# Grouped-query attention: K of a head pair loaded with 8 KB rows, the score matmuls on four tiles, P written with a step of 2

## The chip, the core and the metric

The kernel runs on one core of a Trainium2 chip. The core has five engines that each work through their own list of instructions: PE (TensorE, matmuls and transposes into PSUM), DVE (VectorE), ACT (ScalarE), POOL (GpSimd) and SP (SyncE, which here only issues transfers). They meet at semaphores. Sixteen DMA engines move data between the memory outside (HBM) and the 128 partitions of the on-chip memory (SBUF). The metric is the device time of one execution in microseconds (us). Before the change it is 353.08 us, the median of three runs (351.69 to 353.13).

## The reference: what is computed

```
B, Hq, Hkv, Sq, Sk, D = 16, 32, 8, 16, 2048, 128        # q, k, v in bf16
k = jnp.repeat(k, 4, axis=1); v = jnp.repeat(v, 4, axis=1)
scores = jnp.einsum("bhqd,bhkd->bhqk", q, k) * D ** -0.5
p = softmax(scores, axis=-1)
out = jnp.einsum("bhqk,bhkd->bhqd", p, v)
```

There are 16 x 8 = 128 KV heads. Four query heads of 16 rows share each, so a KV head has a block of 64 query rows against 2048 keys of 128 numbers. K and V of one KV head are 512 KB each; all of K and V is 134 MB, and q and the output are 2 MB each.

## The kernel before

Two KV heads make a *pair*: 64 + 64 query rows fill 128 partitions, and there are `NP` = 64 pairs. All loops run over pairs p.

**Loads (SP, L158 to L206).** For each step t, SP issues K of pair t (`load_k`, L160), every eighth step a block of Q, V of pair t-4 (`load_v`, L170), and the store of the result of pair t-12 (`store`, L190). K has `NK` = 6 buffers `Kn`, V has 8. K of pair p waits until the transposes of pair p-6 are done (L163), V of pair p until PV of pair p-8 is done (L173). The view `kf` (L87) puts head g, partition a at 2048 consecutive numbers, that is 4 KB: partition a of `Kn` holds keys 16a to 16a+15 of the first head and then the same of the second. A transfer of 1 MB thus consists of 256 pieces of 4 KB. K of pair 0 comes as two transfers of 512 KB with a semaphore each (L164 to L166). V has the same layout (L88); V of the last pair comes in two halves of 2 KB rows (L178). The store of a pair writes 128 rows of 256 B.

**Transposes of K (DVE, `kt`, L286).** Scores need K with the 128 numbers of a key along the partitions. DVE transposes 32x32 blocks of 4-byte words (two bf16 at a time), one instruction of 1024 words per partition for each head, from `Kn` to `KT` (two buffers). After it, the partitions 32r to 32r+31 hold the keys that lay in those partitions of `Kn`: block r of 32 partitions has 512 keys of head 0 and 512 of head 1.

**Scores (PE, op "S", L229 to L250).** The query block comes transposed in `QT`, in four slices (`acc`) of 32 numbers each, repeated in every 32-partition block. For each `acc`, 8 matmuls of 32 rows x 64 columns x 512 keys go to 8 different tiles of the PE array: row block r (4 of them) times column half g (head g, 2 of them). Output: bank r of `S_ps`, partition half g. The four `acc` add up in PSUM. S of pair p waits for both transposes of pair p and, since there is only one `S_ps`, for DVE to have read the scores of pair p-1 (`sem_max`).

**Softmax.** DVE copies `S_ps` to `Sneg` (L307), scaled by -scale and with the row minimum into `nbias`. ACT (L336) takes exp of `Sneg` plus bias, sums the rows and writes P in bf16, two neighbours to each 4-byte word. PE transposes P in 4-byte words (op "PT", L259, two halves), ACT copies the result to `PT` (L346). PE multiplies `PT` by V (op "PV", L275, 32 matmuls, three pairs behind), and ACT scales by the reciprocal of the row sum (L356).

**Order.** PE's and ACT's lists are written out by the loop at L115 to L136: PE does S(p+1), PV(p-3), PT(p), and in four of each eight steps a part of the next Q block (QT, L227). DVE's list (L300 to L315) is, for each p: Sneg(p), the reciprocal of p-1 (L298), the two transposes of pair p+2.

Of the kernel before, what the change touches and what calls it, by code (L numbers as in the profile page):

```python
# [5 lines left out]
ACT = mybir.ActivationFunctionType  # L6
ALU = mybir.AluOpType
BF16 = mybir.dt.bfloat16
# [16 lines left out]
def bass_standalone__gqa_softmax__sampling_kernel(  # L25
# [21 lines left out]
    iota_t = sb("iota_t", [128, 128], I32)  # L47
    ident = sb("ident", [128, 128], BF16)
    ident4 = sb("ident4", [128, 128], F32)
    Kn = [sb(f"Kn{i}", [128, 2, J * 128], BF16) for i in range(NK)]  # L50
    Vb = [sb(f"Vb{i}", [128, 2, J, 128], BF16) for i in range(NV)]
    KT = [sb(f"KT{i}", [128, 2, J * 64], F32) for i in range(NKT)]
    Qn = [sb(f"Qn{i}", [128, 8, 128], BF16) for i in range(NQ)]

    QT = [sb(f"QT{i}", [128, 4, 1024], BF16) for i in range(2)]
# [10 lines left out]
    O_ps = ctx.enter_context(nc.psum_tensor("O_ps", [128, 512], F32))  # L66

    sem_id = sem("sem_id")
    sem_k0 = [sem(f"sem_k0{g}") for g in range(2)]
    sem_k = [sem(f"sem_k{i}") for i in range(NK)]  # L70
    sem_v = [sem(f"sem_v{i}") for i in range(NV)]
    sem_vl = [sem(f"sem_vl{i}") for i in range(2)]
# [11 lines left out]

    qf = q.rearrange("b h s d -> (b h s) d")
    of = out.rearrange("b h s d -> (b h s) d")
    kf = k.rearrange("b h s d -> (b h) (s d)").rearrange("g (a x) -> a g x", a=128)  # L87
    vf = v.rearrange("b h s d -> (b h) (s d)").rearrange("g (a x) -> a g x", a=128)  # L88


# [58 lines left out]
    with nc.Block() as block:  # L149
# [8 lines left out]
        @block.sync  # L158
        def _(sp):
            def load_k(p):  # L160
                s = p % NK
                if p >= NK:
                    sp.wait_ge(sem_kt, 2 * (p - NK) + 2)  # L163
                if p == 0:  # L164
                    for g in range(2):
                        sp.dma_start(Kn[s][:, g, :], kf[:, g, :]).then_inc(sem_k0[g], 16)  # L166
                else:
                    sp.dma_start(Kn[s][:, :, :], kf[:, 2 * p:2 * p + 2, :]).then_inc(sem_k[s], 16)  # L168

            def load_v(p):  # L170
                s = p % NV
                if p >= NV:
                    sp.wait_ge(sem_pv, p - NV + 1)  # L173
                if p < NP - 1:
                    dst = Vb[s][:, :, :, :].rearrange("a g j d -> a g (j d)")
                    sp.dma_start(dst, vf[:, 2 * p:2 * p + 2, :]).then_inc(sem_v[s], 16)  # L176
                    return
                for x in range(2):  # L178
                    dst = Vb[s][:, :, 8 * x:8 * (x + 1), :].rearrange("a g j d -> a g (j d)")
                    src = vf[:, 2 * p:2 * p + 2, 1024 * x:1024 * (x + 1)]  # L180
                    sp.dma_start(dst, src).then_inc(sem_vl[x], 16)  # L181

            def load_q(c):
                s = c % NQ
                if c >= NQ:
                    sp.wait_ge(sem_st, last_q[c - NQ, 3] + 1)
                src = qf[1024 * c:1024 * (c + 1), :].rearrange("(a j) d -> a j d", j=8)
                sp.dma_start(Qn[s][:, :, :], src).then_inc(sem_q[s], 16)

            def store(p):  # L190
                s = p % NO
                sp.wait_ge(sem_nm, p + 1)
                sp.dma_start(of[128 * p:128 * (p + 1), :], Osb[s][:, :]).then_inc(sem_o[s], 16)  # L193

            for t in range(NP + SLAG + 1):
                if t < NP:
                    load_k(t)
                for c in range(NQC):
                    if t == max(0, 8 * c - QLEAD):
                        load_q(c)  # L200
                if 0 <= t - VLAG < NP:
                    load_v(t - VLAG)
                if 0 <= t - SLAG < NP:
                    store(t - SLAG)
            for s in range(NO):
                sp.wait_ge(sem_o[s], 16 * (NP // NO))  # L206

        @block.tensor
        def _(pe):
# [6 lines left out]
            for op in pe_prog:  # L216
                if op[0] == "QT":
                    _, c, i, u = op
                    if i == 0:
                        pe.wait_ge(sem_q[c % NQ], 16 * (c // NQ + 1))  # L220
                    free(u)
                    dst = stage_ap(u).bitcast(BF16)
                    src = Qn[c % NQ][:, :, :].rearrange("p j (b c e) -> p j b e c", b=2, e=2)
                    b, e = divmod(i, 2)
                    for j in range(8):
                        for r in range(4):
                            ins = pe.transpose(dst[32 * r:32 * (r + 1), 128 * j:128 * (j + 1)], src[:, j, b, e, :], ident[:, :])  # L227
                    ins.then_inc(sem_st, 1)
                elif op[0] == "S":  # L229
                    _, p = op  # L230
                    pe.wait_ge(sem_kt, 2 * p + 2)
                    if p >= 1:
                        pe.wait_ge(sem_max, p)
                    c, i = divmod(p, 8)
                    if i == 0:
                        pe.wait_ge(sem_ev, last_q[c, 3] + 1)
                    kt = KT[p % NKT][:, :, :].bitcast(BF16).rearrange("p g (t b x e) -> p g b e t x", t=J // 2, b=2, e=2)
                    qt = QT[c % 2]
                    for acc in range(4):
                        b, e = divmod(acc, 2)  # L240
                        for r in range(4):
                            rows = slice(32 * r, 32 * (r + 1))
                            for g in range(2):
                                ins = pe.matmul(  # L244
                                    S_ps[64 * g:64 * (g + 1), 512 * r:512 * (r + 1)],
                                    qt[rows, acc, 128 * i + 64 * g:128 * i + 64 * (g + 1)],
                                    kt[rows, g, b, e, :, :],
                                    start=(acc == 0), stop=(acc == 3),
                                )
                    ins.then_inc(sem_s, 1)  # L250
                elif op[0] == "PT":
                    _, p, h, u = op
                    if h == 0:
                        pe.wait_ge(sem_exp, p + 1)
                    free(u)
                    dst = stage_ap(u)
                    for t in range(4):
                        x = 4 * h + t
                        ins = pe.transpose(dst[:, 128 * t:128 * (t + 1)], P[p % 2][:, 128 * x:128 * (x + 1)], ident4[:, :])  # L259
                    ins.then_inc(sem_st, 1)  # L260
                elif op[0] == "PV":
                    _, p = op
                    pe.wait_ge(sem_ev, last_p[p, 1] + 1)
                    if p < NP - 1:
                        pe.wait_ge(sem_v[p % NV], 16 * (p // NV + 1))
                    if p >= NP - 3:
                        pe.wait_ge(sem_max, NP)
                    elif p >= 1:
                        pe.wait_ge(sem_nm, p)
                    pt = PT[p % NPT][:, :, :].bitcast(BF16).rearrange("p t (q e) -> p t e q", e=2)  # L270
                    for j in range(J):
                        if p == NP - 1 and j % 8 == 0:
                            pe.wait_ge(sem_vl[j // 8], 16)
                        for g in range(2):
                            ins = pe.matmul(  # L275
                                o_ap(p)[64 * g:64 * (g + 1), :],
                                pt[:, j // 2, j % 2, 64 * g:64 * (g + 1)],
                                Vb[p % NV][:, g, j, :],
                                start=(j == 0), stop=(j == J - 1),
                                skip_group_check=True,  # L280
                            )
                    ins.then_inc(sem_pv, 1)

        @block.vector
        def _(dve):
            def kt(p, g):  # L286
                if p == 0:
                    dve.wait_ge(sem_k0[g], 16)
                else:
                    dve.wait_ge(sem_k[p % NK], 16 * (p // NK + (1 if p % NK else 0)))  # L290
                dve.transpose(  # L291
                    KT[p % NKT][:, g, :].rearrange("p (t b a e) -> p t e b a", t=J // 2, b=2, e=2),
                    Kn[p % NK][:, g, :].bitcast(F32).rearrange("p (t e b c) -> p t e b c", e=2, b=2, c=32),
                ).then_inc(sem_kt, 1)

            def recip(p):
# [22 lines left out]
        def _(act):  # L319
            for op in act_prog:  # L320
# [9 lines left out]
                elif op[0] == "exp":  # L330
                    _, p = op
                    act.wait_ge(sem_max, p + 1)
                    if p >= 2:
                        act.wait_ge(sem_st, last_p[p - 2, 1] + 1)

                    act.activation(  # L336
                        P[p % 2][:, :].bitcast(BF16).rearrange("p (t r x) -> p t r x", t=8, r=4),
                        Sneg[p % 2][:, :].rearrange("p (r t x) -> p t r x", t=8, r=4), ACT.Exp,
                        bias=nbias[:, p:p + 1], scale=-1.0, accum_out=rowsum[:, p:p + 1],
                    ).then_inc(sem_exp, 1)  # L340
                elif op[0] == "pe":
# [44 lines left out]
```

## Time and profile before

| | us |
|---|---|
| median of three runs | 353.08 |
| the profiled execution: its time | 352.63 |
| its span, first to last instruction | 350.4 |
| PE busy | 243.3 |
| DVE busy | 296.3 |
| ACT busy | 255.6 |

The mean granted clock of PE is 0.937 of full. 139.22 MB are moved in 45525 packets. The page of the profile has the busy time of each engine, the span in 40 slices (digits are tenths), the DMA queues, the chain of work that ended last, and the groups of instructions with their number, busy time, mean duration in ns, and the idle time before them with what ended it. Other views are the list of waits, the timeline, and a table of stretches of time with the busy time of each engine, the share of DMA time and the rate.

### The profile page before, as it was taken

The page shows a single profiled execution, that of the slowest core. Times are in us where ns is not written, and L with a number is a line of the kernel's source. Part 1 is how long each engine was busy: PE and PEld are TensorE (multiplying, and loading weights), DVE is VectorE, ACT ScalarE, POOL GpSimd, SP SyncE. Part 2 cuts the span into 40 slices and gives each one's busy share as a digit, 9 for nine tenths or more (in the row PEclk, how much of TensorE's full clock was granted, in tenths as well). Part 3 has the DMA queues.
Part 4 walks back from the last instruction along what each step waited for, and adds up shares of the span by engine and source line. Part 5 has one row for each costly group of instructions (what it writes and reads, how often), then busy time and mean ns, then how long its engine had stood idle before and what let it go on. Part 6 is the DMA issues. An engine that isn't in the chain of part 4 may idle for free.

```text
span 350.4 us, 12631 instructions
## 1 busy us (share of the span) xinstructions
PE 243.3 (69%) x5632; PEld 173.5 (50%) x5632; DVE 296.3 (85%) x320; ACT 255.6 (73%) x353; POOL 1.4 (0%) x7
## 2 busy tenths in 40 slices
PE   2578876778667775687649666676775776697675
PEld 2246544546445543365436544454563554465454
DVE  2899999978789887889888897898888888988980
ACT  2578887877758785678757976578957689676575
POOL 1000000000000000000000000000000000000000
PEclk9769999998989999899998999899988999988899
DMA  7999999999999999999999999999999999999983
GB/s 280 416 408 409 406 408 405 412 411 408 414 410 410 412 409 411 410 413 408 408 412 411 409 412 408 410 415 406 411 412 410 410 389 410 412 411 411 409 342 117
DMA packets 45525, 139.22 MB, mean 397 GB/s; under 512 B 11424, under 2 KB 11424, under 8 KB 45472
## 3 DMA queue, kind: packets, MB, share of 16 engines
q1 hardware_dynamic: 45472, 138.42, 99.5%
q8 instruction: 44, 0.72, 0.8%
q14 instruction: 9, 0.07, 0.1%
HBM read 136.31 MB, written 2.10 MB: 395 GB/s over the span
## 4 chain that ended last, share of the span: by engine, by line
DMA 75%; DVE 10%; SPq 6%; issue 5%; PE 2%; ACT 1%
DMA Kn<-in_k_dram 70%; DVE KT L291 8%; DMA Vb<-in_v_dram 4%; SPq L176 3%; DVE Sneg L307 2%; SPq L193 2%; DMA Qn<-in_q_dram 1%; ACT QT L326 1%; SPq L168 1%; PE S_ps L244 1%; PE O_ps L275 0%; PE ST_ps L227 0%; SPq L181 0%; SPq L166 0%; ACT O L356 0%
## 5 line engine op out<-in xcount | busy, mean ns | idle before, releaser
L291 DVE STREAM_TRANSPOSE KT<-Kn 128x1024 f32<-128x1024 f32 x128 | 151.8, 1225 | 43.6 <-DMA Kn<-in_k_dram 43.5
L336 ACT ACTIVATE P<-Sneg,nbias 128x2048 bf16<-128x2048 f32 x64 | 128.1, 2001 | 37.4 <-DVE Sneg L307 37.0
L307 DVE TENSOR_SCALAR_CACHE_REDUCE Sneg<-S_ps 128x2048 f32<-128x2048 f32 x64 | 144.2, 2253 | 1.8 <-PE S_ps L244 1.8
L244 PE MATMUL S_ps<-KT,QT 32*64 32x512 bf16 x2048 | 81.3, 425 | 87.5 <-DVE Sneg L307 75.2
L244 PEld LDWEIGHTS S_ps<-KT,QT 32*64 32x64 bf16 x2048 | 33.7, 109 | 113.5 <-issue 102.7
L346 ACT ACTIVATE PT<-ST_ps 128x512 f32<-128x512 f32 x128 | 69.9, 596 | 21.4 <-PE ST_ps L259 21.4
L259 PE MATMUL ST_ps<-ident,P 128*128 128x128 f32 x512 | 73.1, 288 | 8.9 <-ACT P L336 8.6
L275 PEld LDWEIGHTS O_ps<-Vb,PT 128*64 128x64 bf16 x1952 | 63.1, 119 | 30.3 <-issue 28.8
L275 PE MATMUL O_ps<-Vb,PT 128*64 128x128 bf16 x1952 | 73.7, 233 | 1.2 <-issue 1.0
L259 PEld LDWEIGHTS ST_ps<-ident,P 128*128 128x128 f32 x512 | 57.5, 145 | 18.1 <-ACT P L336 13.6
L356 ACT ACTIVATE O<-O_ps,rrec 128x128 bf16<-128x128 f32 x61 | 22.3, 366 | 25.7 <-PE O_ps L275 25.0
L326 ACT ACTIVATE QT<-ST_ps 128x1024 bf16<-128x1024 bf16 x32 | 32.4, 1024 | 5.6 <-PE ST_ps L227 5.5
L227 PE MATMUL ST_ps<-ident,Qn 128*32 128x128 bf16 x1024 | 21.4, 233 | 6.4 <-DMA Qn<-in_q_dram 6.4
L227 PEld LDWEIGHTS ST_ps<-ident,Qn 128*32 128x32 bf16 x1024 | 16.3, 103 | 11.3 <-issue 10.9
L298 DVE RECIPROCAL rrec<-rowsum 128x1 f32<-128x1 f32 x64 | 10.1, 158 | 2.3 <-ACT P L336 2.3
L336 ACT ACTIVATION_READ_ACCUMULATOR P<-Sneg,nbias 128x1 f32 x64 | 12.1, 188 | 0.0
L307 DVE DVE_READ_ACCUMULATOR Sneg<-S_ps 128x1 f32 x64 | 5.3, 83 | 0.0
L275 PE MATMUL S_ps<-Vb,PT 128*64 128x128 bf16 x96 | 3.4, 220 | 0.7 <-DMA Vb<-in_v_dram 0.6
L275 PEld LDWEIGHTS S_ps<-Vb,PT 128*64 128x64 bf16 x96 | 2.9, 110 | 1.2 <-DMA Vb<-in_v_dram 0.7
L356 ACT ACTIVATE O<-S_ps,rrec 128x128 bf16<-128x128 f32 x3 | 1.1, 369 | 2.0 <-PE S_ps L275 2.0
L326 ACT ACT_TABLE_LOAD x1 | 1.3, 1283 | 0.7 <-PEq L371 0.7
L155 POOL TENSOR_SCALAR ident<-iota_t 128x128 bf16<-128x128 int32 x1 | 0.5, 534 | 0.1
(6 smaller groups left out, 1.2 us busy)
## 6 DMA issues: line engine op xcount, KB each, us to landing
Kn<-in_k_dram SPq DMA_DIRECT2D x63, 1024.0 KB, 15.0
Vb<-in_v_dram SPq DMA_DIRECT2D x63, 1024.0 KB, 16.3
Qn<-in_q_dram SPq DMA_DIRECT2D x8, 256.0 KB, 14.6
out_dram<-O SPq DMA_DIRECT2D x64, 32.0 KB, 13.9
Kn<-in_k_dram SPq DMA_DIRECT2D x2, 512.0 KB, 4.1
Vb<-in_v_dram SPq DMA_DIRECT2D x2, 512.0 KB, 13.4
```

The source lines that it names most:

```text
L176: sp.dma_start(dst, vf[:, 2 * p:2 * p + 2, :]).then_inc(sem_v[s], 16)
L227: ins = pe.transpose(dst[32 * r:32 * (r + 1), 128 * j:128 * (j + 1)], src[:, j, b, e, :], ident[:, :])
L244: ins = pe.matmul(S_ps[64 * g:64 * (g + 1), 512 * r:512 * (r + 1)], qt[rows, acc, 128 * i + 64 * g:128 * i + 64 * (g + 1)], kt[rows, g, b, ...
L259: ins = pe.transpose(dst[:, 128 * t:128 * (t + 1)], P[p % 2][:, 128 * x:128 * (x + 1)], ident4[:, :])
L275: ins = pe.matmul(o_ap(p)[64 * g:64 * (g + 1), :], pt[:, j // 2, j % 2, 64 * g:64 * (g + 1)], Vb[p % NV][:, g, j, :], start=(j == 0), stop ...
L291: dve.transpose(KT[p % NKT][:, g, :].rearrange("p (t b a e) -> p t e b a", t=J // 2, b=2, e=2), Kn[p % NK][:, g, :].bitcast(F32).rearrange ...
L298: dve.reciprocal(rrec[:, p:p + 1], rowsum[:, p:p + 1]).then_inc(sem_rec, 1)
L307: dve.tensor_scalar(Sneg[p % 2][:, :], S_ps[:, :], -scale, None, op0=ALU.mult, op1=ALU.min, accum_out=nbias[:, p:p + 1],).then_inc(sem_max, 1)
L326: act.activation(QT[c % 2][:, i, :].rearrange("p (a j) -> p a j", j=8), stage_ap(u).bitcast(BF16).rearrange("p (j a) -> p a j", j=8), ACT. ...
L336: act.activation(P[p % 2][:, :].bitcast(BF16).rearrange("p (t r x) -> p t r x", t=8, r=4), Sneg[p % 2][:, :].rearrange("p (r t x) -> p t r ...
L346: act.activation(PT[p % NPT][:, 4 * h:4 * (h + 1), :].rearrange("p t q -> p (t q)"), stage_ap(u), ACT.Copy,).then_inc(sem_ev, 1)
L356: act.activation(Osb[p % NO][:, :], o_ap(p), ACT.Copy, scale=rrec[:, p:p + 1]).then_inc(sem_nm, 1)
```

## The change

K of a pair is read as one megabyte that is cut into 128 equal rows: partition a gets 8 KB, that is 32 consecutive keys. The first head fills the partitions 0 to 63, the second 64 to 127. Pair 0 is no longer loaded in two halves, and its two semaphores go. The two transposes of a pair now take the first and the second half of every row (16 of the 32 keys) of both heads, and write every second 4-byte word of `KT`. Row blocks 0 and 1 of `KT` hold only keys of head 0, row blocks 2 and 3 only keys of head 1. So a row block meets only one column half: for each `acc` there are two groups (`u`) of four matmuls of the same size as before, and in a group the row blocks r and r+2 write the same bank of `S_ps`, on different partition halves. Number and sizes of the matmuls stay. The keys lie in another order along `Sneg`; so that P keeps the pairs of neighbours that V's layout asks for, exp writes its bf16 numbers with a step of 2.

```diff
-    Kn = [sb(f"Kn{i}", [128, 2, J * 128], BF16) for i in range(NK)]
+    Kn = [sb(f"Kn{i}", [128, 2 * J * 128], BF16) for i in range(NK)]
-    KT = [sb(f"KT{i}", [128, 2, J * 64], F32) for i in range(NKT)]
+    KT = [sb(f"KT{i}", [128, 2 * J * 64], F32) for i in range(NKT)]
-    kf = k.rearrange("b h s d -> (b h) (s d)").rearrange("g (a x) -> a g x", a=128)
+    kf = k.rearrange("b h s d -> (b h s d)").rearrange("(n a x) -> n a x", n=NP, a=128)
...
-                if p == 0:
-                    for g in range(2):
-                        sp.dma_start(Kn[s][:, g, :], kf[:, g, :]).then_inc(sem_k0[g], 16)
-                else:
-                    sp.dma_start(Kn[s][:, :, :], kf[:, 2 * p:2 * p + 2, :]).then_inc(sem_k[s], 16)
+                sp.dma_start(Kn[s][:, :], kf[p]).then_inc(sem_k[s], 16)
...
-                    kt = KT[p % NKT][:, :, :].bitcast(BF16).rearrange("p g (t b x e) -> p g b e t x", t=J // 2, b=2, e=2)
+                    kt = KT[p % NKT][:, :].bitcast(BF16).rearrange("p (t b y e) -> p b e t y", t=J // 2, b=2, e=2)
...
-                        for r in range(4):
-                            rows = slice(32 * r, 32 * (r + 1))
-                            for g in range(2):
+                        for u in range(2):
+                            for r in range(4):
+                                rows = slice(32 * r, 32 * (r + 1))
+                                g, h = divmod(r, 2)
                                 ins = pe.matmul(
-                                    S_ps[64 * g:64 * (g + 1), 512 * r:512 * (r + 1)],
+                                    S_ps[64 * g:64 * (g + 1), 512 * (2 * h + u):512 * (2 * h + u + 1)],
                                     qt[rows, acc, 128 * i + 64 * g:128 * i + 64 * (g + 1)],
-                                    kt[rows, g, b, e, :, :],
+                                    kt[rows, b, e, 4 * u:4 * (u + 1), :],
                                     start=(acc == 0), stop=(acc == 3),
                                 )
...
-            def kt(p, g):
-                if p == 0:
-                    dve.wait_ge(sem_k0[g], 16)
-                else:
-                    dve.wait_ge(sem_k[p % NK], 16 * (p // NK + (1 if p % NK else 0)))
+            def kt(p, x):
+                dve.wait_ge(sem_k[p % NK], 16 * (p // NK + 1))
                 dve.transpose(
-                    KT[p % NKT][:, g, :].rearrange("p (t b a e) -> p t e b a", t=J // 2, b=2, e=2),
-                    Kn[p % NK][:, g, :].bitcast(F32).rearrange("p (t e b c) -> p t e b c", e=2, b=2, c=32),
+                    KT[p % NKT][:, :].rearrange("p (t b e a x) -> p x e t b a", t=J // 2, b=2, e=2, x=2)[:, x, :, :, :, :],
+                    Kn[p % NK][:, :].bitcast(F32).rearrange("p (x t e b c) -> p x e t b c", x=2, e=2, b=2, c=32)[:, x, :, :, :, :],
                 ).then_inc(sem_kt, 1)
...
-                        P[p % 2][:, :].bitcast(BF16).rearrange("p (t r x) -> p t r x", t=8, r=4),
-                        Sneg[p % 2][:, :].rearrange("p (r t x) -> p t r x", t=8, r=4), ACT.Exp,
+                        P[p % 2][:, :].bitcast(BF16).rearrange("p (t h y e) -> p t h e y", t=8, h=2, e=2),
+                        Sneg[p % 2][:, :].rearrange("p (h t e y) -> p t h e y", t=8, h=2, e=2), ACT.Exp,
```

More of the change, by code (lines that the diff above doesn't have):

```diff
@@ L68, in bass_standalone__gqa_softmax__sampling_kernel @@
     sem_id = sem("sem_id")
-    sem_k0 = [sem(f"sem_k0{g}") for g in range(2)]
     sem_k = [sem(f"sem_k{i}") for i in range(NK)]
```

## The prediction

> **What bounds the kernel now.** I read the page's first three parts, then the chain that ended last, the groups and the waits, and last two tables: the timeline of single pairs and the rates of stretches of time. The page (busy time, slices, queue, chain):
>
> ```profile
> PE 243.3 (69%) x5632; PEld 173.5 (50%) x5632; DVE 296.3 (85%) x320; ACT 255.6 (73%) x353; POOL 1.4 (0%) x7
> ...
> DMA  7999999999999999999999999999999999999983
> ...
> DMA packets 45525, 139.22 MB, mean 397 GB/s; under 512 B 11424, under 2 KB 11424, under 8 KB 45472
> ...
> q1 hardware_dynamic: 45472, 138.42, 99.5%
> ...
> DMA 75%; DVE 10%; SPq 6%; issue 5%; PE 2%; ACT 1%
> ```
>
> The DMA engines are full from the second slice to the 38th, and 75% of the chain is loads. No compute engine is full; DVE is nearest. All 45472 packets are under 8 KB: by pieces, 16384 for K, 16384 + 256 for V, 1024 for Q, 8192 of 256 B for the stores, and 16 small ones for each of the 202 transfers make exactly that number. The waits confirm the chain:
>
> ```profile
> DVE KT L291 <- DMA Kn<-in_k_dram: 43.5, 54, 4.4
> ```
>
> DVE, the busiest engine, idles 43.5 us in total for K to land. The groups that the change touches:
>
> ```profile
> L291 DVE STREAM_TRANSPOSE KT<-Kn 128x1024 f32<-128x1024 f32 x128 | 151.8, 1225 | 43.6 <-DMA Kn<-in_k_dram 43.5
> L336 ACT ACTIVATE P<-Sneg,nbias 128x2048 bf16<-128x2048 f32 x64 | 128.1, 2001 | 37.4 <-DVE Sneg L307 37.0
> L307 DVE TENSOR_SCALAR_CACHE_REDUCE Sneg<-S_ps 128x2048 f32<-128x2048 f32 x64 | 144.2, 2253 | 1.8 <-PE S_ps L244 1.8
> L244 PE MATMUL S_ps<-KT,QT 32*64 32x512 bf16 x2048 | 81.3, 425 | 87.5 <-DVE Sneg L307 75.2
> ```
>
> And the table of stretches (length, busy time of PE, PEld, DVE, ACT, POOL, then PE's clock, DMA share, GB/s). Up to 48 us no store runs yet; from 60 to 280 us everything runs; after 334 us K has all landed and only V and stores are left, and near 338 us V comes in its 2 KB rows:
>
> ```profile
> 18.00:48.00 30.00, 23.57 (x543) 15.83 (x544) 30.00 (x35) 25.36 (x35) 0.00 (x0) 0.91 1.03 408
> 60.00:280.00 220.00, 153.94 (x3624) 110.08 (x3624) 189.71 (x206) 164.23 (x226) 0.00 (x0) 0.95 1.03 410
> 334.00:336.00 2.00, 2.00 (x48) 1.76 (x40) 2.00 (x3) 1.60 (x4) 0.00 (x0) 1.00 1.02 393
> 336.00:338.00 2.00, 0.10 (x1) 0.00 (x0) 2.00 (x3) 0.82 (x3) 0.00 (x0) 1.00 1.02 386
> ```
>
> A pair moves 2.163 MB (K and V 2.097, store and its share of Q 0.033 each); at 410 GB/s that is 5.28 us. This is the period, set by the transfers. So an edit counts if it changes the transfer rate, or if it pushes the compute loop above 5.28 us.
>
> **The change part by part.**
>
> *Transfers of K.* 256 pieces of 4 KB become 128 of 8 KB; each of the 16 DMA engines has 8 pieces fewer per pair, 512 over 64 pairs. The bytes stay. What a piece costs beyond its bytes no row gives alone, so I bound it. Loads of 4 KB at 408 GB/s are 25.5 GB/s per engine, 160.6 ns for a piece. Lower end: in the steady stretch an engine's 32 loads and 8 stores of a pair (133120 B at 25.6 GB/s) take 5195 ns; less 32 x 160.6 = 5139, that leaves 7 ns for a store of 256 B, which at 25.5 GB/s has 10 ns in its bytes alone: nothing fixed. Upper end: at 334 to 336 us, 16 loads and 8 stores (67584 B at 24.6 GB/s) take 2752 ns; less 2570 that is 23 ns a store, 13 ns fixed. Nearest to the change is the 336 to 338 stretch, loads with the row length halved: at 386 GB/s two pieces of 2 KB take 169.8 ns against 160.6 for one of 4 KB, so 9.2 ns a piece (the stretch is not purely such rows, hence both ends stay). 512 x 9.2 ns = 4.7 us gained; the ends are 0 and 512 x 13 = 6.6 us. A loss isn't excluded either: no row shows a piece over 4 KB. The slowest full slice of the steady part moves 389 GB/s; if K went at that, its 64 x 16 x 160.6 ns = 164.5 us would grow by 410/389, 8.9 us.
>
> [...]
>
> *Pair 0 in one transfer.* DVE starts its first transposes at 4.41 us, done at 6.9; with the whole megabyte to wait for, at most one half's 1.3 us later. S(0) starts at 11.42 behind the Q chain, and DVE idles 2.72 us before the transposes of pair 1. Nothing.
>
> *Scores.* The timeline of a pair at full clock and of one at half clock (start, duration):
>
> ```profile
> 151.66 1.11 PE L244 MATMUL S_ps<-KT,QT 32*64 32x512 bf16 x32
> ...
> 151.96 2.37 DVE L291 STREAM_TRANSPOSE KT<-Kn 128x1024 f32<-128x1024 f32 x2 [0.50 <-DMA Kn<-in_k_dram]
> ...
> 154.26 2.25 DVE L307 TENSOR_SCALAR_CACHE_REDUCE Sneg<-S_ps 128x2048 f32<-128x2048 f32 x1
> ```
> ```profile
> 19.53 1.93 PE L244 MATMUL S_ps<-KT,QT 32*64 32x512 bf16 x32 [0.47 <-DVE Sneg L307]
> ```
>
> Eight tiles at once make four rounds of 512 columns. 1.11 us at full and 1.93 at half clock give 0.82 us for four rounds and 0.29 fixed. Four tiles at once make eight rounds: 0.29 + 1.64 = 1.93 us, and 3.57 at half clock. The cover is DVE, which between two Sneg does the reciprocal and two transposes: S may take from 151.66 to 154.26, 2.60 us, and even where DVE waited for nothing (S at 24.06, next Sneg at 26.18) 2.12. So 0.82 us more is hidden at full clock. On PE, PV stands behind S and PT behind PV: PV (1.13 us, at 152.70) moves to 153.5, ends at 154.65, and PT waits for exp until 154.84 anyway. A step with a Q part adds to 1.93 + 1.13 + 1.09 + 0.63 = 4.8 us, under 5.28. At half clock S passes the cover by about 1 us; a mean clock of 0.937 is half clock in 12.6% of the time, 8 pairs, 8 us of lateness for DVE against its 43.5 us of idle. SP isn't reached by this: a load lands 15 us after its issue, so three pairs are always queued, and K's buffer was free three pairs before. Cost taken: 0; upper end 8 us.
>
> [...]
>
> *Transposes.* The same 1024 words each, read in runs of 64, written in the same step of two words, in runs of 32 where it was 64. No row shows that; taken as 0, since count and step stay. DVE has 0.68 us idle per pair, so it decides from 1225 to 1560 ns on; doubled, DVE's 4.63 us per pair become 7.08, and the end 352.6 + 64 x 1.8 = 468 us. A shorter transpose gains nothing while K is awaited.
>
> *Exp with a step of 2.* The only stepped ACT row is the Q copy (it reads in steps): 1024 numbers in 1024 ns, 1.00 ns each, against 0.98 for exp. Taken as 0. ACT is busy 4.0 us of 5.28 per pair; doubled to 4.0 us, exp makes it 6.0, and 352.6 + 64 x 0.7 = 397. A gain is off the path.
>
> *End.* PV of the last pair waits for V at 347.38; without that wait it would have gone on at about 346.1. S(63) at the end isn't covered: 0.8 us later, still inside. Nothing.
>
> Sum against the profiled execution: 352.6 - 4.7 = 347.9; it lies 0.45 under the median, so 348.4 for a median.
>
> **The rivals.** *The rate doesn't depend on the row length* (the pieces are cut into 4 KB, or fetching runs ahead): 353, nothing hidden being exposed. For it: stores of 256 B leave the steady rate at 410. Against: 386 and 393 in the end stretches. *Scores become the bound* (slower): the loop Sneg 2.33, hand-over 0.28, S must stay under 5.28, so it decides when S passes 2.67 us. If the two tiles that share a bank take turns, S has sixteen rounds, 3.57 us, the period is 6.18, and start 13.4 + 63 x 6.18 + tail 11 = 414 us. In a milder form, half-clock lateness that isn't absorbed, 353 + 8 = 361. Against: 1.93 is well below 2.67. *8 KB rows are slower*: up to 8.9 us, 362, the middle 357. For it only that no row shows such pieces. *DVE or ACT dislikes the new steps*: 397 to 468.
>
> **How the numbers follow.** This kernel's measurement tells about 0.5% (1.8 us) from no change. Chances: forecast 0.45 (346 to 351); rate unchanged 0.21; slower rows 0.13; half-clock lateness 0.11; shared banks 0.05; steps 0.05. Faster is the forecast, 0.45; same 0.21; slower the rest, 0.34. The range begins at 345.8, the upper end of the gain (353.1 - 6.6 = 346.5) and a little, and reaches to 358, which takes in the unchanged rate, the middle of the slower rows and most of the lateness; the last tenth and a little more lies above.
>
> **What would show it.** Packets on the queue fall by 8192 + 16 to 37264 with 8192 no longer under 8 KB (if they stay near 45456, pieces are cut and the forecast falls); the rate of the steady stretch goes from 410 to about 416; S takes 1.93 us at full clock, and Sneg still waits for PE hardly at all; transposes stay at 1225 ns, exp at 2001. Wrong it would be if Sneg waits on S, if DVE's wait for K goes to nothing, or if the rate falls.

## The result, and the profile after

The changed kernel takes 349.62 us (348.95 to 350.27, four runs) against 353.11 us (351.69 to 353.6, four runs) before: a ratio of 0.9905, 95% interval 0.9878 to 0.9932. That is 3.5 us less, where 4.7 were forecast. The profiled execution takes 348.95 us and spans 347.2.

The page of the changed kernel: busy times, DMA slices, packets, queue, and the chain by engine.

```profile
PE 283.2 (82%) x5632; PEld 192.3 (55%) x5632; DVE 296.2 (85%) x320; ACT 285.8 (82%) x353; POOL 1.5 (0%) x7
...
DMA  7999999999999999999999999999999999999983
...
DMA packets 37316, 139.21 MB, mean 401 GB/s; under 512 B 11408, under 2 KB 11408, under 8 KB 29072
...
q1 hardware_dynamic: 37264, 138.42, 98.7%
...
DMA 34%; ACT 20%; PE 15%; DVE 12%; issue 12%; SPq 5%; ACTq 0%
```

The queue carries the forecast 37264 packets, and 8192 of them are no longer under 8 KB: the 8 KB rows travel whole. The DMA engines are as full as before, so the same bytes went through faster. The table of stretches says how much (the last number is GB/s):

```profile
18.00:48.00 30.00, 24.61 (x472) 15.62 (x468) 27.56 (x31) 24.89 (x32) 0.00 (x0) 0.97 1.02 414
60.00:280.00 220.00, 187.94 (x3760) 126.81 (x3760) 196.80 (x216) 189.44 (x235) 0.00 (x0) 0.98 1.03 415
```

415 stands where 410 stood, and 414 where 408 did. But loads are only 34% of the chain now, where they were 75%; ACT and PE, 1% and 2% before, hold 35%. The groups that the change touches:

```profile
L329 ACT ACTIVATE P<-Sneg,nbias 128x2048 bf16<-128x2048 f32 x64 | 167.0, 2609 | 13.3 <-DVE Sneg L300 12.9
L284 DVE STREAM_TRANSPOSE KT<-Kn 128x1024 f32<-128x1024 f32 x128 | 151.4, 1221 | 30.0 <-DMA Kn<-in_k_dram 29.9
L240 PE MATMUL S_ps<-KT,QT 32*64 32x512 bf16 x2048 | 131.2, 392 | 34.7 <-DVE Sneg L300 31.7
L300 DVE TENSOR_SCALAR_CACHE_REDUCE Sneg<-S_ps 128x2048 f32<-128x2048 f32 x64 | 144.8, 2263 | 12.6 <-PE S_ps L240 12.2
```

The transposes cost what they did (1221 ns against 1225). Exp did not stay: 2609 ns against 2001. Sneg now waits 12.2 us in all for the scores, 1.8 before, and DVE's wait for K falls from 43.5 to 29.9 us. The scores, which took 1.11 us for a pair, take 2.00 (the timelines below show it). Two parts of the computation have become longer, then, and the question is what of that is paid for.

### The profile page after: what moved, and what is told of

Same layout as the page of the kernel before. It is cut to its first block, busy times and chain, and to the rows that moved or that the text cites. A ratio compares the mean times of both kernels' runs of the same rounds, so it can differ in the third digit from the quotient of the medians.

```text
span 347.2 us, 12630 instructions
## 1 busy us (share of the span) xinstructions
PE 283.2 (82%) x5632; PEld 192.3 (55%) x5632; DVE 296.2 (85%) x320; ACT 285.8 (82%) x353; POOL 1.5 (0%) x7
## 3 DMA queue, kind: packets, MB, share of 16 engines
q1 hardware_dynamic: 37264, 138.42, 98.7%
## 4 chain that ended last, share of the span: by engine, by line
DMA 34%; ACT 20%; PE 15%; DVE 12%; issue 12%; SPq 5%; ACTq 0%
DMA Kn<-in_k_dram 33%; ACT P L329 14%; DVE Sneg L300 7%; PE S_ps L240 7%; DVE KT L284 5%; PE ST_ps L255 5%; ACT PT L339 4%; SPq L188 4%; PE O_ps L271 2%; DMA Qn<-in_q_dram 1%; ACT QT L319 1%; PE S_ps L271 1%; SPq L171 1%; ACT O L349 1%; SPq L163 0%
## 5 line engine op out<-in xcount | busy, mean ns | idle before, releaser
L329 ACT ACTIVATE P<-Sneg,nbias 128x2048 bf16<-128x2048 f32 x64 | 167.0, 2609 | 13.3 <-DVE Sneg L300 12.9
L284 DVE STREAM_TRANSPOSE KT<-Kn 128x1024 f32<-128x1024 f32 x128 | 151.4, 1221 | 30.0 <-DMA Kn<-in_k_dram 29.9
L240 PE MATMUL S_ps<-KT,QT 32*64 32x512 bf16 x2048 | 131.2, 392 | 34.7 <-DVE Sneg L300 31.7
L300 DVE TENSOR_SCALAR_CACHE_REDUCE Sneg<-S_ps 128x2048 f32<-128x2048 f32 x64 | 144.8, 2263 | 12.6 <-PE S_ps L240 12.2
L240 PEld LDWEIGHTS S_ps<-KT,QT 32*64 32x64 bf16 x2048 | 61.3, 104 | 83.9 <-issue 44.5
L255 PE MATMUL ST_ps<-ident,P 128*128 128x128 f32 x512 | 70.3, 280 | 20.2 <-ACT P L329 19.8
L255 PEld LDWEIGHTS ST_ps<-ident,P 128*128 128x128 f32 x512 | 55.1, 141 | 30.5 <-ACT P L329 28.5
L271 PEld LDWEIGHTS O_ps<-Vb,PT 128*64 128x64 bf16 x1952 | 57.1, 111 | 26.5 <-issue 26.5
L271 PE MATMUL O_ps<-Vb,PT 128*64 128x128 bf16 x1952 | 67.1, 222 | 0.0
```

The source lines that it names most:

```text
L240: ins = pe.matmul(S_ps[64 * g:64 * (g + 1), 512 * (2 * h + u):512 * (2 * h + u + 1)], qt[rows, acc, 128 * i + 64 * g:128 * i + 64 * (g + 1 ...
L271: ins = pe.matmul(o_ap(p)[64 * g:64 * (g + 1), :], pt[:, j // 2, j % 2, 64 * g:64 * (g + 1)], Vb[p % NV][:, g, j, :], start=(j == 0), stop ...
L284: dve.transpose(KT[p % NKT][:, :].rearrange("p (t b e a x) -> p x e t b a", t=J // 2, b=2, e=2, x=2)[:, x, :, :, :, :], Kn[p % NK][:, :].b ...
L300: dve.tensor_scalar(Sneg[p % 2][:, :], S_ps[:, :], -scale, None, op0=ALU.mult, op1=ALU.min, accum_out=nbias[:, p:p + 1],).then_inc(sem_max, 1)
L329: act.activation(P[p % 2][:, :].bitcast(BF16).rearrange("p (t h y e) -> p t h e y", t=8, h=2, e=2), Sneg[p % 2][:, :].rearrange("p (h t e ...
```

## The experiments

**Long rows alone, and the new compute alone.** The change has two halves that can be taken apart: how K travels, and what PE and ACT do with it. The first kernel is the one before with this edit, with which pair 0 also comes in one transfer and DVE's waits are numbered as in the changed kernel:

```diff
...
-    kf = k.rearrange("b h s d -> (b h) (s d)").rearrange("g (a x) -> a g x", a=128)
+    kf = k.rearrange("b h s d -> (b h s d)").rearrange("(n a x) -> n a x", n=NP, a=128)
...
-                    sp.dma_start(Kn[s][:, :, :], kf[:, 2 * p:2 * p + 2, :]).then_inc(sem_k[s], 16)
+                sp.dma_start(Kn[s][:, :, :].rearrange("a g x -> a (g x)"), kf[p]).then_inc(sem_k[s], 16)
...
```

> The kernel before with K in 8 KB rows and nothing else of the change (the keys are then matched to the wrong heads, so part of the computation is changed; all instructions are as before). Theory A, a fixed price of about 9 ns for each piece: 512 fewer pieces per engine, 348.4 us, steady rate 415 to 416 GB/s at a PE clock near 0.94. Theory B, the gain comes from the longer scores, which keep PE at a higher clock (0.985 after against 0.937) and DVE on time: here 353 us, 410 GB/s.

The second is the changed kernel with the old `kf` and this transfer:

```diff
-                sp.dma_start(Kn[s][:, :], kf[p]).then_inc(sem_k[s], 16)
+                sp.dma_start(Kn[s][:, :].rearrange("a (g x) -> a g x", g=2), kf[:, 2 * p:2 * p + 2, :]).then_inc(sem_k[s], 16)
```

> The changed kernel with K loaded in 4 KB pieces as before, all its compute kept (keys matched to the wrong heads). Theory A: the transfers bound it as before, 410 GB/s, 353 us, up to 1.2 us more for the two exps of 2.6 us that lie open at the end. Theory B: 349.6 us as the changed kernel, clock 0.985.

Measured: long rows alone 348.17 us, ratio 0.9871 (0.9847 to 0.9894), rate 415 GB/s at a clock of 0.936; new compute alone 353.75 us, ratio 1.0024 (1.0007 to 1.0041), rate 410 at a clock of 0.984. Both stood beside the kernel before at 352.69. The steady stretch of the first and of the second:

```profile
60.00:280.00 220.00, 161.74 (x3704) 114.42 (x3708) 193.44 (x211) 165.54 (x231) 0.00 (x0) 0.92 1.03 415
```
```profile
60.00:280.00 220.00, 185.43 (x3696) 125.42 (x3696) 194.15 (x209) 186.35 (x233) 0.00 (x0) 0.98 1.03 410
```

Theory B falls: the clock goes with the new compute, the time with the rows. The rows are worth 4.5 us (3.7 to 5.4 by the interval), which is 8.8 ns for each of the 512 pieces fewer per engine. The new compute costs 1.1 us (0.2 to 1.4).

**The other direction.** K of a pair (but the first) in two transfers of 2 KB rows:

```diff
-                    sp.dma_start(Kn[s][:, :, :], kf[:, 2 * p:2 * p + 2, :]).then_inc(sem_k[s], 16)
+                    for x in range(2):
+                        cols = slice(1024 * x, 1024 * (x + 1))
+                        sp.dma_start(Kn[s][:, :, cols], kf[:, 2 * p:2 * p + 2, cols]).then_inc(sem_k[s], 16)
...
-                    dve.wait_ge(sem_k[p % NK], 16 * (p // NK + (1 if p % NK else 0)))
+                    dve.wait_ge(sem_k[p % NK], 32 * (p // NK + (1 if p % NK else 0)))
```

> The kernel before with K in two transfers of 2 KB rows per pair, the other direction: 1024 more pieces per engine. Theory A at 9.2 ns a piece: 9.4 us more, 362.5 us, steady rate about 399 GB/s; at 13 ns 366. No fixed price: 353 us, 410 GB/s.

Measured: 361.27 us against 352.69, ratio 1.0245 (1.0215 to 1.0275). Sixteen pieces more in 63 pairs make 1008 per engine, so 8.5 ns a piece. The edit also makes 63 more transfers, each with one more small packet per engine; counted as pieces too, they bring it to 8.0 ns. The same two stretches of this kernel:

```profile
18.00:48.00 30.00, 23.56 (x533) 15.68 (x531) 29.84 (x35) 25.13 (x35) 0.00 (x0) 0.90 1.04 397
60.00:280.00 220.00, 152.63 (x3510) 108.90 (x3508) 185.28 (x201) 159.65 (x220) 0.00 (x0) 0.93 1.04 399
```

Two sizes on either side of 4 KB give the same price within the intervals (8.8 and 8.5 ns), so from 2 to 8 KB a fixed cost per piece describes the loads.

The traces also hold the duration of every single packet, and these show the price directly. Between 60 and 280 us the median packet takes 309 ns for 8 KB and 159 ns for 4 KB in the changed kernel, and 159 ns for 4 KB and 84 ns for 2 KB in the kernel with short rows. Two of half the length cost 9 ns more than one, both times. In the kernel before, the stores of 256 B take 18 ns and the small packets of 4 B take 9. All of these are 9 ns and the bytes at 75 ns for 2 KB. For 512 pieces that makes 4.6 us, beside the 4.5 measured.

**V in long rows too.** The changed kernel with V's transfers as contiguous megabytes:

```diff
-    vf = v.rearrange("b h s d -> (b h) (s d)").rearrange("g (a x) -> a g x", a=128)
+    vf = v.rearrange("b h s d -> (b h s d)").rearrange("(n a x) -> n a x", n=NP, a=128)
...
-                    dst = Vb[s][:, :, :, :].rearrange("a g j d -> a g (j d)")
-                    sp.dma_start(dst, vf[:, 2 * p:2 * p + 2, :]).then_inc(sem_v[s], 16)
+                    dst = Vb[s][:, :, :, :].rearrange("a g j d -> a (g j d)")
+                    sp.dma_start(dst, vf[p]).then_inc(sem_v[s], 16)
...
```

> The changed kernel with V in 8 KB rows as well (V then meets the wrong keys; instructions otherwise as in the changed kernel). Theory A, 8.7 ns for each of another 512 pieces per engine: 4.4 us less, 345.2 us, steady rate about 420 GB/s. Rival, the rate is near its ceiling or the compute loop near 5.2 us per pair: no more than 1 us gained, 348.6 or more, with DVE's wait for K close to nothing.

The last V keeps its two halves, so 504 pieces per engine go and not the 512 of the expectation. Measured: 346.33 us (beside the kernel before at 352.19, ratio 0.983, 0.9807 to 0.9852), steady rate 419:

```profile
60.00:280.00 220.00, 188.14 (x3817) 127.68 (x3819) 199.82 (x219) 191.57 (x239) 0.00 (x0) 1.00 1.02 419
```

That is 3.3 us under the changed kernel, or 2.6 by the ratios of the two to the kernel before in their own series of runs, where 4.4 were expected: most of the step comes again. DVE still waits 27.8 us for K, so the compute loop isn't the bound. Nor is a piece cheaper than thought: here too the median packet of 8 KB takes 309 ns. Why a quarter or more of the gain is missing wasn't settled.

**What the new compute costs, and where.** If exp's 0.6 us and the scores' 0.9 were paid in each of 64 pairs, it would be 96 us; 1.1 was measured. The timelines of the last pairs show the place (start, duration). Long rows alone:

```profile
334.27 1.11 PE L239 MATMUL S_ps<-KT,QT 32*64 32x512 bf16 x32 [1.74 <-DVE Sneg L299]
...
335.46 2.29 DVE L299 TENSOR_SCALAR_CACHE_REDUCE Sneg<-S_ps 128x2048 f32<-128x2048 f32 x1 [1.26 <-PE S_ps L239]
...
337.99 2.01 ACT L328 ACTIVATE P<-Sneg,nbias 128x2048 bf16<-128x2048 f32 x1
...
340.14 1.09 PE L254 MATMUL ST_ps<-ident,P 128*128 128x128 f32 x8 [0.81 <-ACT P L328]
...
341.17 2.31 PE L270 MATMUL S_ps<-Vb,PT 128*64 128x128 bf16 x64
```

The changed kernel:

```profile
334.22 2.00 PE L240 MATMUL S_ps<-KT,QT 32*64 32x512 bf16 x32 [1.04 <-DVE Sneg L300]
...
336.26 2.29 DVE L300 TENSOR_SCALAR_CACHE_REDUCE Sneg<-S_ps 128x2048 f32<-128x2048 f32 x1 [2.12 <-PE S_ps L240]
...
338.83 2.58 ACT L329 ACTIVATE P<-Sneg,nbias 128x2048 bf16<-128x2048 f32 x1
...
341.51 1.09 PE L255 MATMUL ST_ps<-ident,P 128*128 128x128 f32 x8 [1.34 <-ACT P L329]
...
342.53 1.98 PE L271 MATMUL S_ps<-Vb,PT 128*64 128x128 bf16 x64
```

From the start of the last scores to the start of the last transposes it is 5.87 us in the one and 7.29 in the other, 1.42 more: 0.89 from the scores, 0.57 from exp. No transpose of K is left to cover them. And the PV of the last two pairs (64 matmuls) runs through in one piece, 1.98 us, without a wait for V. In the kernel before, the last pair had to wait for V:

```profile
344.97 1.83 PE L275 MATMUL S_ps<-Vb,PT 128*64 128x128 bf16 x48
...
347.38 0.64 PE L275 MATMUL S_ps<-Vb,PT 128*64 128x128 bf16 x16 [0.58 <-DMA Vb<-in_v_dram]
```

The landings in the traces say why that wait went away. Before, the last V lands 14.0 us after the last K (347.33 and 333.34). From that K it is 11.63 us of compute to the start of PV and, at 1.98 us for 64 matmuls, 1.49 more to its last quarter, 13.1 in all; so V sets the end, by 0.9 us. With the long rows alone the compute is the same 11.63, but V lands 13.0 us after K (342.55 and 329.54): no wait is left. In the changed kernel the compute is 13.05 + 1.49 = 14.5 us and V lands 13.3 us after K (342.80 and 329.48), so about 1.2 us of compute lie open behind the last V. The long rows thus bring the last V closer to the last K, and the new compute comes on top of that.

**Ending behind V again.** If that open end is the loss, K should come a little earlier and V stay: `VLAG = 5` in place of 4, that is V issued five steps behind K.

```diff
-VLAG = 4
+VLAG = 5
```

> The changed kernel with V issued five steps behind K instead of four, so the last K lands about one pair (5.2 us) earlier and the last V when it did. If the open compute behind the last K sets the end of the changed kernel, as theory A has it, the end moves to the landing of the last V: 347.5 to 348.5 us. If the transfers set the end anyway: 349.6.

> The kernel before with V five steps behind K. There the last PV waited for V at 347.38 us, so the compute behind the last K was covered: 352.7 us, no change. If it gains as much as the changed kernel does, the open compute isn't what the changed kernel lost.

> The same with six steps. Theory A: nothing further over five steps, since the last V already sets the end: 347.5 to 348.5 us; PV may begin to wait for V in the steady part, which would make it 349 or more.

Measured, beside the kernel before at 352.14: the changed kernel takes 348.2 us with five steps, ratio 0.9886 (0.9871 to 0.99); the kernel before with five steps 352.21, ratio 0.9997 (0.9984 to 1.0009), no change; the changed kernel with six steps 349.62, ratio 0.9921 (0.9904 to 0.9938). Between the medians the changed kernel gains 1.4 us from the fifth step. It was measured in another series of runs, though: by the ratios to the kernel before it is 0.7 us, with intervals that overlap, and by the two profiled executions 0.6. The old kernel gains nothing, as it must be if only the changed one ended in open compute. The end of the five-step kernel shows the wait for V back:

```profile
340.91 1.71 PE L271 MATMUL S_ps<-Vb,PT 128*64 128x128 bf16 x48
...
343.22 0.64 PE L271 MATMUL S_ps<-Vb,PT 128*64 128x128 bf16 x16 [0.60 <-DMA Vb<-in_v_dram]
```

The last K lands 1.9 us earlier there (327.56 against 329.48 us), not the 5.2 of the expectation, and the last V 0.4 later (343.18 against 342.80). So the changed kernel with five steps is the fastest here that computes what the reference does, by a little; the long rows alone, equally fast, are no alternative, since there the keys meet the wrong heads. Six steps lose it again: the last PV no longer waits for V, and the waits of the whole span are these (us in total, times, longest):

```profile
DVE Sneg L300 <- PE S_ps L240: 35.7, 39, 3.3
...
PE O_ps L271 <- issue: 24.0, 28, 2.5
...
DVE KT L284 <- DMA Kn<-in_k_dram: 6.5, 2, 5.7
```

Sneg waited 20.0 us for scores with five steps. The wait of PE before PV has no releaser in this view, but the landings name it: in 29 of the first 63 pairs PV starts within 0.25 us of the landing of its V (27 with five steps, none with four, where V is always there at least 1.57 us before). So PE, which does PV between the scores, now waits for V in the steady part, and the scores are late. Five steps pay part of this price already.

**Exp without its step.** Two ways to let exp write neighbours in order. In the first, PE reads the moving K so that the scores come out in that order:

```diff
-                    kt = KT[p % NKT][:, :].bitcast(BF16).rearrange("p (t b y e) -> p b e t y", t=J // 2, b=2, e=2)
+                    kt = KT[p % NKT][:, :].bitcast(BF16).rearrange("p (t b w y e) -> p b e t y w", t=J // 2, b=2, w=2, e=2)
...
-                        P[p % 2][:, :].bitcast(BF16).rearrange("p (t h y e) -> p t h e y", t=8, h=2, e=2),
-                        Sneg[p % 2][:, :].rearrange("p (h t e y) -> p t h e y", t=8, h=2, e=2), ACT.Exp,
+                        P[p % 2][:, :].bitcast(BF16).rearrange("p (t h x) -> p t h x", t=8, h=2),
+                        Sneg[p % 2][:, :].rearrange("p (h t x) -> p t h x", t=8, h=2), ACT.Exp,
```

> The changed kernel, but PE reads the moving K so that the scores of neighbouring keys come out next to each other; exp then writes P without a step. Theory A: exp goes from 2609 back to about 2000 ns; hidden in the steady part, 0.6 us for each of the two exps that lie open at the end, so 348.4 us. Rival: the end is set by the last V anyway, 349.6. If PE's reading order is dear, S passes 2.1 us and Sneg waits for it.

In the second, with the same exp as in the first (not shown again), DVE's transposes write the words in that order:

```diff
-                    KT[p % NKT][:, :].rearrange("p (t b e a x) -> p x e t b a", t=J // 2, b=2, e=2, x=2)[:, x, :, :, :, :],
+                    KT[p % NKT][:, :].rearrange("p (t b a x e) -> p x e t b a", t=J // 2, b=2, e=2, x=2)[:, x, :, :, :, :],
...
```

> The changed kernel, but the transposes of K write the words in another order (a step of four words instead of two), so that neighbouring keys come out of the scores next to each other and exp writes P without a step; PE reads as in the changed kernel. Theory A: of the 1.45 us by which the changed kernel stays behind the one with long rows alone, 0.6 is the exp of the last pair and 0.9 its scores; exp back at 2000 ns gives 349.0 us. If the wider step is dear for DVE (over 1560 ns for each transpose) the time rises above 353; if exp is hidden at the end too, 349.6.

Both put exp back at 2.0 us and lose far more elsewhere. The first takes 471.71 us, ratio 1.3375 (1.3341 to 1.3409); one round of its pairs, and the wait of Sneg:

```profile
201.50 4.51 PE L240 MATMUL S_ps<-KT,QT 32*64 32x512 bf16 x32 [0.45 <-DVE Sneg L300]
...
206.05 2.29 DVE L300 TENSOR_SCALAR_CACHE_REDUCE Sneg<-S_ps 128x2048 f32<-128x2048 f32 x1 [2.36 <-PE S_ps L240]
```

Scores of 4.51 us are past the 2.67 at which the prediction let them become the bound, and the loop is Sneg 2.33 + hand-over 0.28 + S 4.51 = 7.12 us; the trace has 7.00 from one Sneg (at 199.05) to the next. The second takes 404.8 us, ratio 1.1484 (1.1452 to 1.1516):

```profile
L284 DVE STREAM_TRANSPOSE KT<-Kn 128x1024 f32<-128x1024 f32 x128 | 252.0, 2073 | 5.6 <-DMA Kn<-in_k_dram 5.6
```

Transposes of 2073 ns put DVE's pair at 4.63 + 2 x 0.85 = 6.33 us. The trace has 6.02 on average from one Sneg to the next (60 to 280 us), since two transposes in a row take 3.98 us and not 4.15, and DVE is busy all of that time. 63 such periods are 379 us; 15 before the first Sneg and 11 from the start of the last make the rest. Of these three places for the step, ACT is the cheapest.

**Two row blocks in one bank.** For head 1 the two groups of scores change places, so that the four matmuls of a group write four banks:

```diff
                                 g, h = divmod(r, 2)
+                                w = 1 - u if g else u
...
-                                    S_ps[64 * g:64 * (g + 1), 512 * (2 * h + u):512 * (2 * h + u + 1)],
+                                    S_ps[64 * g:64 * (g + 1), 512 * (2 * h + w):512 * (2 * h + w + 1)],
...
-                                    kt[rows, b, e, 4 * u:4 * (u + 1), :],
+                                    kt[rows, b, e, 4 * w:4 * (w + 1), :],
```

> The changed kernel with the two groups of scores exchanged for head 1, so that the four matmuls of a group write four different banks. If two row blocks in one bank cost something, S falls from 2.00 us (towards 1.93); if not, S stays at 2.00. The time stays at 349.6 us either way.

Measured: 349.86 us in the one run that was made, and S again 2.00 us. The minimum, median and maximum of one (ns), of this kernel between 100 and 300 us:

```profile
L241 PE MATMUL S_ps<-KT,QT x1248: 380/382/631, 100.1 to 298.7; 32*64 32x512 bf16 x179
```

and of the changed kernel:

```profile
L240 PE MATMUL S_ps<-KT,QT x1236: 380/382/630, 99.6 to 299.1; 32*64 32x512 bf16 x177
```

The matmuls take the same time. Sharing a bank on different partition halves costs nothing here.

## Why the prediction was right, and where not

*Transfers.* This was right in place and size: 9.2 ns a piece was forecast, 8.8 and 8.5 were measured, and the rate went to 415 where 416 was forecast. That the number came out so close is luck. The stretch from 336 to 338 us was read as loads with halved rows, with the caution that it isn't purely such rows. By the packet records of that trace, rows of 2 KB take only 42% of the engines' time in it, and rows of 4 KB 52%. That "no row gives alone" the cost of a piece holds for the views, but the packets of the kernel before gave it: 9, 18, 84 and 159 ns for 4 B, 256 B, 2 KB and 4 KB. The two bounds, 0 and 13, came from stretches with stores of 256 B; the lower one, "nothing fixed", is wrong, as these stores take 9 ns beyond their bytes too.

*Scores.* Eight rounds were put at 1.93 us; 2.00 was measured. The cover held in most pairs, but "Sneg waits on S" was named as a sign of being wrong, and 12.2 us of it came. Of these, 5.2 fall before 60 us, 5.0 in eight waits between 60 and 280 us, and 2.1 at the last pair. In the steady part DVE still waits 18.0 us for K, so that lateness lies inside a loop that has K to wait for. The feared lateness at half clock went the other way: the granted clock rose from 0.937 to 0.985. The long rows alone (0.936) and the new compute alone (0.984) show that it goes with the new compute. PE is busy 283.2 us with the longer scores, where it was 243.3; whether that is the reason for the clock was not shown.

*Shared banks.* Turns at a shared bank, with S at 3.57 us, had a chance of 0.05. S took 2.00 us with and without sharing, and the median matmul 382 ns both times.

*Transposes and pair 0.* The transposes are unchanged at 1221 ns. The first ones start at 5.61 us where 5.7 was allowed, and S(0) starts at 11.39.

*Exp.* Here the first step failed: "Taken as 0", from a row that reads in steps and writes in order. A write in steps is another thing: 30% on top, 0.61 us. It is off the path in 63 pairs, as the text had it for a longer exp, since ACT, busy 4.5 us per pair (285.8 / 64), stays under the period of 5.2. Of the rivals, "DVE or ACT dislikes the new steps" was true in kind for ACT, and far below the doubling that it was priced at.

*End.* The step that failed is "still inside. Nothing." The cover by the last V was put at 1.3 us, of which the scores were to use 0.8. It was 0.9: PV would have gone on at 346.46 (344.97 and three quarters of 1.98), not at 346.1. Exp was missing from the sum; with its 0.57 and the 0.89 of the scores it is 1.46, more than the cover. The cover had also gone by itself, as the long rows alone show with the old compute. So the prediction counted 4.7 of gain where 4.5 came, and some 1.2 us were given back at the end: 1.2 by the landings of the changed kernel, 1.1 by the new compute against the kernel before, 1.4 by the changed kernel against the long rows alone (another series; 1.1 by the spans of their profiles). Five steps in place of four, 0.6 to 1.4, agree with it but tell it less exactly. That accounts for the difference between 348.4 and 349.6.

*Rivals.* An unchanged rate, slower rows and scores as the bound were excluded by the 415 GB/s and the DVE waits; two kernels built for another purpose then showed what the scores and the transposes as the bound look like, 472 and 405 us.

## What to carry to other kernels

Where loads are the bound, count pieces as well as bytes: a cost of some 9 ns for each piece on each DMA engine forecasts the gain of the longer rows here. Where the trace keeps single packets, compare their times at two sizes before reading whole stretches. Then walk the last pair by itself with every changed duration in it: what is hidden in 63 rounds lies open in the 64th, and the wait that covered it may move with the gain. If the end turns from waiting for a load to open compute, change the order of the loads by one step before touching the compute.

## What was not expected of the hardware

- DMA: a packet takes 9 ns and its bytes at 75 ns for 2 KB, from 4 B (9 ns) over 256 B (18), 2 KB (84) and 4 KB (159) to 8 KB (309).
- ACT: exp that writes 2-byte numbers at a step of 4 bytes takes 2609 ns for 2048 against 2000 in order.
- DVE: the 32x32 transposes of 1024 words take 1221 ns with a step of two words in the destination and 2073 with four.
- PE: when the moving columns alternate between places 256 B apart, a round of 512 columns takes 0.54 us, by the distance from one group of weight loads to the next, instead of 0.21, which is (2.00 - 0.29) / 8; the scores as a whole 4.51 instead of 2.00. Why these steps on ACT, DVE and PE cost what they do was not shown.
- The DMA engines don't end together. In the changed kernel their mean share is 0.90 at 334 to 336 us and then falls to 0.59 and 0.55 until 340:

```profile
334.00:336.00 2.00, 1.78 (x32) 0.99 (x32) 0.14 (x3) 1.90 (x1) 0.00 (x0) 1.00 0.90 332
336.00:338.00 2.00, 2.00 (x44) 1.77 (x40) 1.74 (x1) 1.27 (x4) 0.00 (x0) 1.00 0.59 226
338.00:340.00 2.00, 2.00 (x67) 1.83 (x65) 0.64 (x3) 2.00 (x3) 0.00 (x0) 1.00 0.55 205
```

Nearly half of the engines' time is unused there, for some 6 us (0.48 from 340 to 342). The kernel before shows the same from 340 to 346 (0.57, 0.59, 0.55). The landings tell more: each transfer has 16 of them, taken here as one per engine. The 16 of the last V come in two groups, eight from 335.3 to 336.0 us and eight from 341.1 to 342.8. The engines had drifted apart during the run: the landings of one K transfer lie 0.3 us apart for pair 1, 4.9 for pair 32 (160.55 to 165.41) and 9.1 for pair 63 (320.37 to 329.48). So DVE waits for the slower eight, and these alone set when the last V is there. Which engines they are, and why they are slower, stays open.
